# Grouped-query attention: V in 8 KB rows, PV in 64x64 tiles, and another pairing of the heads

## The chip, the cores and the metric

The kernel runs on one core of one Trainium2 chip. The metric is device time in microseconds (us) of one launch; less is better. The kernel is bound to data that comes from memory (HBM) into the on-chip SBUF over 16 DMA engines, and works on five engines: TensorE (PE, matmuls and transposes into PSUM), VectorE (DVE), ScalarE (ACT), GpSimd (POOL) and SyncE (SP, which issues the DMAs here).

## The reference

Attention with grouped queries. There are 16 batches, 8 key/value heads each with 2048 positions of 128 elements, and 32 query heads with 16 positions; four query heads share a key/value head, so 64 query rows meet each K and V head.

```python
B, Hq, Hkv, Sq, Sk, D = 16, 32, 8, 16, 2048, 128      # all bfloat16
k = jnp.repeat(k, rep, axis=1)                        # rep = Hq // Hkv = 4
v = jnp.repeat(v, rep, axis=1)
scale = D ** -0.5
scores = jnp.einsum("bhqd,bhkd->bhqk", q, k) * scale
p = _softmax(scores, axis=-1)
return jnp.einsum("bhqk,bhkd->bhqd", p, v)
```

K and V are 64 MB each and are read once; Q and the output are 2 MB each.

## The kernel before

The 128 key/value heads are taken in 64 pairs, p = 0 to 63. A pair has 2 x 64 query rows, which fill the 128 partitions of a score tile.

**Loads (SP, L180 to L225).** `load_k` brings a pair's K as one DMA of 1 MB: 128 rows of 8 KB, so that partition a of a head holds 32 consecutive positions (`Kn`, six buffers). `load_v` brings a pair's V as 128 partitions x 2 heads x 4 KB (`Vb`, eight buffers), the last pair in two halves. `load_q` brings Q for four pairs in rows of 1 KB, `store` writes 32 KB of output in rows of 256 B. One loop over t issues in order K(t), Q, V(t-5), output(t-12). Each issue waits in this order on SP for its buffer: K for `sem_kt` (K transposed), V for `sem_pv` (PV done), a store for `sem_nm` (output normalized).

**DVE (L338 to L370).** For each pair it turns the score tile into `Sneg` with the row's minimum of the negated scores (L360, `tensor_scalar`), takes the reciprocal of a row sum (`recip`, L351), and transposes the K of two pairs ahead in 32x32 blocks into `KT` (L342, two instructions of 1024 columns).

**PE (L227 to L336).** A program written out by hand (`pe_prog`, L119 to L141): in step p come the scores of pair p+1 ("S", L273 and L232, 32 matmuls of 512 columns in 32x64 tiles, the second half of them on weights that are already loaded), PV of pair p-3 ("PV", L301, 32 matmuls of 128 columns in 128x64 tiles), the transposes of P of pair p ("PT", L284, eight of 128x128), and in two steps of four the transposes of Q ("QT", L251). Eight steps form the body of a loop of seven rounds; four steps before it, three after it and the tail are written out. The waits are on semaphores, in the loop against registers (`at`, `v_at`). Scores have one PSUM tile of four banks (`S_ps`), so S(p+1) waits for DVE's pass over S(p) (`sem_max`). P and Q transposes have three PSUM banks (`ST_ps`), one of them for Q alone.

**ACT (L372 to L411)** follows `act_prog`: exp of pair p (L390, which writes P and the row sum), the normalizing copy of the output of pair p-3 (L410, "norm"), two copies of transposed P into `PT` (L400, "pe"), and copies of transposed Q (L380, "qe").

**POOL (L164)** builds the identity tiles and spreads each Q load into `Q4` (L175).

**The end.** After the loop and three more steps, the tail orders PV 60, PV 61, exp 63, PV 62, the transposes of P 63, PV 63 and the last norms (L131 to L141).

Of the kernel before, what the change touches and what calls it, by code (L numbers as in the profile page):

```python
# [11 lines left out]
NK = 6  # L12
NV = 8
NKT = 2
NPT = 4
NO = 8
NQ = 2
QPAIRS = 4
BODY = 8
VLAG = 5  # L20
PVLAG = 3
SLAG = 12
QLEAD = 7


def bass_standalone__gqa_softmax__sampling_kernel(
# [5 lines left out]
):  # L32
    B, Hq, Sq, D = q.shape
# [3 lines left out]
    G = B * Hkv  # L37
    NP = G // 2
    J = Sk // 128
    assert J == 16 and NP % BODY == 0 and BODY % (2 * QPAIRS) == 0  # L40
    NQC = NP // QPAIRS
# [7 lines left out]
    ident = sb("ident", [128, 128], BF16)  # L49
    ident4 = sb("ident4", [128, 128], F32)  # L50
    Kn = [sb(f"Kn{i}", [128, 2 * J * 128], BF16) for i in range(NK)]
    Vb = [sb(f"Vb{i}", [128, 2, J, 128], BF16) for i in range(NV)]
    KT = [sb(f"KT{i}", [128, 2 * J * 64], F32) for i in range(NKT)]
    Qn = [sb(f"Qn{i}", [128, QPAIRS, 128], BF16) for i in range(NQ)]
    Q4 = sb("Q4", [128, QPAIRS, 2, 4, 64], BF16)
    QT = [sb(f"QT{i}", [128, 2, 128 * QPAIRS], F32) for i in range(2)]
    Sneg = [sb(f"Sneg{i}", [128, Sk], F32) for i in range(2)]
    P = [sb(f"P{i}", [128, Sk // 2], F32) for i in range(2)]
    PT = [sb(f"PT{i}", [128, J // 2, 128], F32) for i in range(NPT)]
    Osb = [sb(f"O{i}", [128, 128], BF16) for i in range(NO)]  # L60
    nbias = sb("nbias", [128, NP], F32)
    rowsum = sb("rowsum", [128, NP], F32)
    rrec = sb("rrec", [128, NP], F32)

    S_ps = ctx.enter_context(nc.psum_tensor("S_ps", [128, Sk], F32))
    ST_ps = ctx.enter_context(nc.psum_tensor("ST_ps", [128, 3 * 512], F32))
    O_ps = ctx.enter_context(nc.psum_tensor("O_ps", [128, 512], F32))
# [4 lines left out]
    sem_vl = [sem(f"sem_vl{i}") for i in range(2)]  # L72
# [10 lines left out]
    sem_ev = sem("sem_ev")  # L83
    sem_nm = sem("sem_nm")

    qf = q.rearrange("b h s d -> (b h s) d")
    of = out.rearrange("b h s d -> (b h s) d")
    kf = k.rearrange("b h s d -> (b h s d)").rearrange("(n a x) -> n a x", n=NP, a=128)
    vf = v.rearrange("b h s d -> (b h) (s d)").rearrange("g (a x) -> a g x", a=128)
# [3 lines left out]
    stages = []  # L93
# [5 lines left out]
    def q_part(c, b):  # L99
        u = stage("Q", c, b)  # L100
        pe_prog.append(("QT", c, b, u))
        act_prog.append(("qe", c, b, u))

    def pv(p):
        pe_prog.append(("PV", p))

    def norm(p):
        act_prog.append(("norm", p))

    def transposes(p):  # L110
        for h in range(2):
            u = stage("P", p, h)
            pe_prog.append(("PT", p, h, u))
            act_prog.append(("pe", p, h, u))

    step_at = {}
    for b in range(2):
        q_part(0, b)
    pe_prog.append(("S", 0))  # L119
    for p in range(NP - 1):  # L120
        step_at[p] = len(pe_prog)
        pe_prog.append(("S", p + 1))
        act_prog.append(("exp", p))
        if p >= PVLAG:
            pv(p - PVLAG)
            norm(p - PVLAG)
        transposes(p)
        c, i = divmod(p, QPAIRS)
        if c + 1 < NQC and i < 2:
            q_part(c + 1, i)  # L130
    tail_at = len(pe_prog)  # L131
    for p in range(NP - 4, NP - 2):
        pv(p)
    act_prog.append(("exp", NP - 1))
    for p in range(NP - 4, NP - 2):
        norm(p)
    pv(NP - 2)
    norm(NP - 2)
    transposes(NP - 1)
    pv(NP - 1)  # L140
    norm(NP - 1)  # L141
    last_q = {what[1:]: u for u, what in enumerate(stages) if what[0] == "Q"}
    last_p = {what[1:]: u for u, what in enumerate(stages) if what[0] == "P"}

    first = PVLAG + 1
    rounds = (NP - 1 - first) // BODY
    assert first % QPAIRS == 0
    after = first + rounds * BODY
    loop_from, loop_to = step_at[first], step_at[first + BODY]
    assert after + 3 == NP - 1  # L150

    def stage_ap(what):
        x = what[2] if what[0] == "P" else 2
        return ST_ps[:, 512 * x:512 * (x + 1)]

    def o_ap(p):
        if p < NP - 3:
            return O_ps[:, 0:128]
        x = p - (NP - 3)
        return S_ps[:, 512 * x:512 * x + 128]  # L160

    with nc.Block() as block:

        @block.gpsimd  # L164
        def _(gp):
# [3 lines left out]
            gp.tensor_scalar(ident4[:, :], iota_t[:, :], 0.0, None, op0=ALU.is_equal).then_inc(sem_id, 1)  # L169
            for c in range(NQC):  # L170
                gp.wait_ge(sem_q[c % NQ], 16 * (c // NQ + 1))
                if c >= 1:
                    gp.wait_ge(sem_st, last_q[c - 1, 1] + 1)
                src = Qn[c % NQ][:, :, :].rearrange("p j (b x) -> p (j b) x", b=2)
                gp.tensor_copy(  # L175
                    Q4[:, :, :, :, :].rearrange("p j b r x -> p (j b) r x"),
                    src.unsqueeze(2).to_broadcast([128, 2 * QPAIRS, 4, 64]),
                ).then_inc(sem_q4, 1)

        @block.sync  # L180
        def _(sp):
            def load_k(p):
                s = p % NK
                if p >= NK:
                    sp.wait_ge(sem_kt, p - NK + 1)
                sp.dma_start(Kn[s][:, :], kf[p]).then_inc(sem_k[s], 16)  # L186

            def load_v(p):
                s = p % NV
                if p >= NV:  # L190
                    sp.wait_ge(sem_pv, p - NV + 1)
                if p < NP - 1:
                    dst = Vb[s][:, :, :, :].rearrange("a g j d -> a g (j d)")
                    sp.dma_start(dst, vf[:, 2 * p:2 * p + 2, :]).then_inc(sem_v[s], 16)
                    return
                for x in range(2):
                    dst = Vb[s][:, :, 8 * x:8 * (x + 1), :].rearrange("a g j d -> a g (j d)")
                    src = vf[:, 2 * p:2 * p + 2, 1024 * x:1024 * (x + 1)]
                    sp.dma_start(dst, src).then_inc(sem_vl[x], 16)
# [9 lines left out]
            def store(p):  # L209
                s = p % NO  # L210
                sp.wait_ge(sem_nm, p + 1)
                sp.dma_start(of[128 * p:128 * (p + 1), :], Osb[s][:, :]).then_inc(sem_o[s], 16)  # L212

            for t in range(NP + SLAG + 1):
                if t < NP:
                    load_k(t)
                for c in range(NQC):
                    if t == max(c, QPAIRS * c - QLEAD):
                        load_q(c)
                if 0 <= t - VLAG < NP:  # L220
                    load_v(t - VLAG)
                if 0 <= t - SLAG < NP:
                    store(t - SLAG)
            for s in range(NO):
                sp.wait_ge(sem_o[s], 16 * (NP // NO))  # L225

        @block.tensor  # L227
        def _(pe):
            pe.wait_ge(sem_id, 3)
# [10 lines left out]
            def emit(op, at, v_at):  # L240

                if op[0] == "QT":
                    _, c, b, u = op
                    if b == 0:
                        pe.wait_ge(sem_q4, at(QPAIRS * c, QPAIRS))
                    if u == 1:
                        pe.wait_ge(sem_ev, 1)
                    dst = stage_ap(op)
                    src = Q4[:, :, :, :, :].bitcast(F32).rearrange("p j b r c -> p j b (r c)")
                    for j in range(QPAIRS):  # L250
                        ins = pe.transpose(dst[:, 128 * j:128 * (j + 1)], src[:, j, b, :], ident4[:, :])  # L251
                    ins.then_inc(sem_st, 1)
                elif op[0] == "S":
                    _, p = op
                    pe.wait_ge(sem_kt, at(p + 1))
                    if p >= 1:
                        pe.wait_ge(sem_max, at(p))
                    c, i = divmod(p, QPAIRS)
                    if p == 0:
                        pe.wait_ge(sem_ev, last_q[0, 1] + 1)  # L260
                    kt = KT[p % NKT][:, :].bitcast(BF16).rearrange("p (t b y e) -> p b e t y", t=J // 2, b=2, e=2)
                    qt = QT[c % 2][:, :, :].bitcast(BF16).rearrange("p b (n e) -> p b e n", e=2)
                    for acc in range(4):
                        b, e = divmod(acc, 2)
                        for u in range(2):
                            for r in range(4):
                                rows = slice(32 * r, 32 * (r + 1))
                                g, h = divmod(r, 2)
                                s_ap = S_ps[64 * g:64 * (g + 1), 512 * (2 * h + u):512 * (2 * h + u + 1)]
                                w = qt[rows, b, e, 128 * i + 64 * g:128 * i + 64 * (g + 1)]  # L270
                                x = kt[rows, b, e, 4 * u:4 * (u + 1), :]
                                if u == 0:
                                    ins = pe.matmul(s_ap, w, x, start=(acc == 0), stop=(acc == 3))  # L273
                                else:
                                    ins = matmul_on_loaded(s_ap, w, x, (32 * r, 64 * g), acc == 0, acc == 3)
                    ins.then_inc(sem_s, 1)
                elif op[0] == "PT":
                    _, p, h, u = op
                    if h == 0:
                        pe.wait_ge(sem_exp, at(p + 1))  # L280
                    dst = stage_ap(("P", p, h))
                    for t in range(4):
                        x = 4 * h + t
# [156 lines left out]
```

## Time and profile before

| what | value |
|---|---|
| three timed runs | 342.7, 342.88, 344.7 us; median 342.88 us |
| profiled execution: its own time, its span | 344.2 us, 342.4 us |
| busy: PE, DVE, ACT, POOL | 82%, 86%, 78%, 9% of the span |
| DMA | 138.63 MB, mean 405 GB/s, 38433 packets |
| K loads | 64 of 1024 KB, 15.9 us from issue to landing (median) |
| V loads | 63 of 1024 KB, 16.5 us; 2 of 512 KB, 12.4 us |
| Q loads, stores | 16 of 128 KB, 15.3 us; 64 of 32 KB, 15.4 us |
| PE waiting for V in front of PV | 36.6 us in 40 waits |
| DVE waiting for K in front of the transpose | 27.8 us in 41 waits |
| granted TensorE clock | 0.994 on average |

The span reaches from the first to the last instruction. In the profile an engine line gives busy time, its share of the span and the number of instructions; the slice line gives the busy share of 40 equal slices in tenths (9 is 90% or more); a timeline line gives start, duration, engine, line of the kernel, operation, output and inputs, and in brackets how long the engine had been idle and what ended that idle time. "SPq" is an issuing instruction on SP.

### The profile page before, as it was taken

What the parts mean: (1) busy time and instruction counts of PE and PEld (TensorE: products, weight loads), DVE (VectorE), ACT (ScalarE), POOL (GpSimd) and SP (SyncE); (2) the same over time, 40 slices, a digit from 0 to 9 for tenths busy, and PEclk for the clock granted to TensorE, in tenths of its full rate; (3) what the DMA queues carried; (4) which work ended last, traced back from release to release, by engine and by line L of the source; (5) the groups of instructions that cost most, each with busy time, mean ns of one, the idle gap of its engine ahead of it and who ended that gap; (6) DMA issues with size and microseconds to landing.
All of it is one profiled execution on the core that took longest, in us unless ns stands there. A gap on an engine that the chain in (4) does not pass through costs nothing.

```text
span 342.4 us, 9887 instructions
## 1 busy us (share of the span) xinstructions
PE 279.9 (82%) x4736; PEld 162.4 (47%) x3712; DVE 295.1 (86%) x320; ACT 267.2 (78%) x353; POOL 31.8 (9%) x23
## 2 busy tenths in 40 slices
PE   0677999999999978879788788878879778798785
PEld 0133555555455644535544544535536445455454
DVE  2489999999999998898898888988988979988940
ACT  1178889999888978878788697796887778787792
POOL 3202020202010010202002020020200102000000
PEclk9999999999999999999999999999999999999997
DMA  7999999999999999999999999999999999999993
GB/s 296 421 409 415 415 408 413 416 413 418 413 415 421 413 418 416 412 419 418 412 421 412 417 417 416 418 417 417 414 419 415 418 414 416 420 419 416 414 409 107
DMA packets 38433, 138.63 MB, mean 405 GB/s; under 512 B 11536, under 2 KB 13584, under 8 KB 30224
## 3 DMA queue, kind: packets, MB, share of 16 engines
q1 hardware_dynamic: 38416, 138.43, 100.0%
q8 instruction: 8, 0.13, 0.2%
q14 instruction: 9, 0.07, 0.1%
HBM read 136.31 MB, written 2.10 MB: 404 GB/s over the span
## 4 chain that ended last, share of the span: by engine, by line
DMA 53%; DVE 20%; issue 9%; SPq 8%; PE 8%; ACT 2%; POOL 1%
DMA Vb<-in_v_dram 47%; DVE KT L342 13%; DVE Sneg L360 6%; SPq L186 6%; DMA Kn<-in_k_dram 5%; PE O_ps L301 3%; SPq L212 2%; PE S_ps L273 1%; DMA Qn<-in_q_dram 1%; PE S_ps L232 1%; ACT O L410 1%; PE S_ps L301 1%; PE ST_ps L251 1%; PE ST_ps L284 1%; POOL Q L175 1%
## 5 line engine op out<-in xcount | busy, mean ns | idle before, releaser
L342 DVE STREAM_TRANSPOSE KT<-Kn 128x1024 f32<-128x1024 f32 x128 | 151.4, 1222 | 27.8 <-DMA Kn<-in_k_dram 27.8
L390 ACT ACTIVATE P<-Sneg,nbias 128x2048 bf16<-128x2048 f32 x64 | 159.6, 2494 | 6.3 <-DVE Sneg L360 6.3
L360 DVE TENSOR_SCALAR_CACHE_REDUCE Sneg<-S_ps 128x2048 f32<-128x2048 f32 x64 | 144.4, 2256 | 7.9 <-PE S_ps L232 7.9
L273 PE MATMUL S_ps<-KT,QT 32*64 32x512 bf16 x1024 | 106.0, 395 | 8.0 <-DVE Sneg L360 6.2
L232 PE MATMUL S_ps<-KT,QT 32*64 32x512 bf16 x1024 | 105.0, 388 | 0.0
L301 PE MATMUL O_ps<-Vb,PT 128*64 128x128 bf16 x1952 | 66.2, 221 | 36.6 <-DMA Vb<-in_v_dram 36.6
L301 PEld LDWEIGHTS O_ps<-Vb,PT 128*64 128x64 bf16 x1952 | 56.5, 110 | 78.8 <-issue 43.9
L400 ACT ACTIVATE PT<-ST_ps 128x512 f32<-128x512 f32 x128 | 69.6, 595 | 20.3 <-PE ST_ps L284 20.3
L284 PE MATMUL ST_ps<-ident,P 128*128 128x128 f32 x512 | 70.8, 282 | 4.1 <-ACT P L390 3.3
L273 PEld LDWEIGHTS S_ps<-KT,QT 32*64 32x64 bf16 x1024 | 32.5, 105 | 72.8 <-issue 62.1
L284 PEld LDWEIGHTS ST_ps<-ident,P 128*128 128x128 f32 x512 | 55.5, 142 | 13.4 <-ACT P L390 9.2
L175 POOL COPY Q<-Qn 128x2048 bf16<-128x2048 bf16 x16 | 30.3, 1896 | 255.6 <-PE ST_ps L251 251.8
L410 ACT ACTIVATE O<-O_ps,rrec 128x128 bf16<-128x128 f32 x61 | 22.5, 369 | 34.1 <-PE O_ps L301 33.9
L251 PE MATMUL ST_ps<-ident,Q 128*128 128x128 f32 x128 | 20.2, 282 | 8.8 <-POOL Q L175 8.1
L380 ACT ACTIVATE QT<-ST_ps 128x512 f32<-128x512 f32 x32 | 19.3, 603 | 8.4 <-PE ST_ps L251 8.4
L251 PEld LDWEIGHTS ST_ps<-ident,Q 128*128 128x128 f32 x128 | 15.5, 145 | 9.1 <-issue 8.0
L390 ACT ACTIVATION_READ_ACCUMULATOR P<-Sneg,nbias 128x1 f32 x64 | 13.2, 207 | 0.0
L351 DVE RECIPROCAL rrec<-rowsum 128x1 f32<-128x1 f32 x64 | 10.2, 159 | 3.0 <-ACT P L390 3.0
L301 PE MATMUL S_ps<-Vb,PT 128*64 128x128 bf16 x96 | 3.9, 243 | 2.7 <-DMA Vb<-in_v_dram 1.6
L360 DVE DVE_READ_ACCUMULATOR Sneg<-S_ps 128x1 f32 x64 | 5.4, 84 | 0.0
L301 PEld LDWEIGHTS S_ps<-Vb,PT 128*64 128x64 bf16 x96 | 3.4, 125 | 3.4 <-issue 2.3
L410 ACT ACTIVATE O<-S_ps,rrec 128x128 bf16<-128x128 f32 x3 | 1.1, 370 | 3.4 <-PE S_ps L301 3.4
(8 smaller groups left out, 3.0 us busy)
## 6 DMA issues: line engine op xcount, KB each, us to landing
Kn<-in_k_dram SPq DMA_DIRECT2D x64, 1024.0 KB, 15.9
Vb<-in_v_dram SPq DMA_DIRECT2D x63, 1024.0 KB, 16.5
Qn<-in_q_dram SPq DMA_DIRECT2D x16, 128.0 KB, 15.3
out_dram<-O SPq DMA_DIRECT2D x64, 32.0 KB, 15.4
Vb<-in_v_dram SPq DMA_DIRECT2D x2, 512.0 KB, 12.4
```

Of the source, the lines that this page charges most:

```text
L175: gp.tensor_copy(Q4[:, :, :, :, :].rearrange("p j b r x -> p (j b) r x"), src.unsqueeze(2).to_broadcast([128, 2 * QPAIRS, 4, 64]),).then_i ...
L186: sp.dma_start(Kn[s][:, :], kf[p]).then_inc(sem_k[s], 16)
L232: return pe.add_instruction(mybir.InstMatmult(name=nc.get_next_instruction_name(), engine=mybir.EngineType.PE, ins=[pe.lower_ap(rhs), pe.l ...
L251: ins = pe.transpose(dst[:, 128 * j:128 * (j + 1)], src[:, j, b, :], ident4[:, :])
L273: ins = pe.matmul(s_ap, w, x, start=(acc == 0), stop=(acc == 3))
L284: ins = pe.transpose(dst[:, 128 * t:128 * (t + 1)], P[p % 2][:, 128 * x:128 * (x + 1)], ident4[:, :])
L301: ins = pe.matmul(o_ap(p)[64 * g:64 * (g + 1), :], pt[:, j // 2, j % 2, 64 * g:64 * (g + 1)], Vb[p % NV][:, g, j, :], start=(j == 0), stop ...
L342: ins = dve.transpose(KT[p % NKT][:, :].rearrange("p (t b e a x) -> p x e t b a", t=J // 2, b=2, e=2, x=2)[:, x, :, :, :, :], Kn[p % NK][: ...
L360: dve.tensor_scalar(Sneg[p % 2][:, :].rearrange("p (t h x) -> p h t x", t=8, h=2), S_ps[:, :].rearrange("p (h t x) -> p h t x", t=8, h=2), ...
L390: act.activation(P[p % 2][:, :].bitcast(BF16).rearrange("p (n y e) -> p n y e", n=16, e=2), Sneg[p % 2][:, :].rearrange("p (n e y) -> p n ...
L400: act.activation(PT[p % NPT][:, 4 * h:4 * (h + 1), :].rearrange("p t q -> p (t q)"), stage_ap(("P", p, h)), ACT.Copy,).then_inc(sem_ev, 1)
L410: act.activation(Osb[p % NO][:, :], o_ap(p), ACT.Copy, scale=rrec[:, p:p + 1]).then_inc(sem_nm, 1)
```

## The change

Two pairs now form a quad d (32 quads of four heads), and a unit u = 2d + i replaces the pair p. Unit i of a quad has the heads {0, 2} (i = 0) or {1, 3} (i = 1) of the quad.

- **K**: the same 1 MB and the same 8 KB rows for a unit, but from two pieces of memory, 64 rows of each of two heads that are not neighbours. One DMA instruction is built by hand whose source is 2 x 64 rows and whose target is 128 partitions. There are seven buffers instead of six. DVE transposes it with one instruction instead of two.
- **V**: a DMA brings two neighbouring heads as 128 rows of 8 KB, so a head lies in 64 partitions. Three buffers of a quad (two loads each) replace eight of a pair. The V of the last quad goes into K buffers that have come free, its last load in rows of 24 and 8 blocks (`LASTJ`).
- **PV**: with a head in 64 partitions, a matmul is 64x64 with 128 columns; there are 128 to a quad, in two halves of 64 in two steps, and the two row halves i write different PSUM banks (`O_ps` has two).
- **P**: exp of the two units of a quad writes interleaved blocks of 64 columns, so that a transpose of 128 columns yields both units. The transposes of a quad follow in two steps, one step later than before; PV follows four steps behind instead of three. P has three buffers of a quad.
- **Q**: 32 loads of 64 KB in rows of 512 B instead of 16 of 128 KB in rows of 1 KB; four transposes and one copy for each. `ST_ps` has two banks instead of three, Q's transposes share a bank with P's, and "QW" is a wait on PE until ACT has copied Q out of it.
- **PE's loop**: six steps in the body, ten rounds, six steps before it; the steps at the end are in the loop too, under branches that skip what isn't there any more. The PV of the last quad follows the loop, in three passes.
- **Output**: a store has 64 partitions x 2 x 256 B; the last quad is normalized by ACT (i = 0) and DVE (i = 1) beside each other.

The core of the diff:

```diff
+NK = 7
+NV = 3
+NO = 6
+NQ = 4
+NQT = 3
+NP = 3
+QPAIRS = 2
+BODY = 6
+FIRST = 6
 VLAG = 5
-PVLAG = 3
-SLAG = 12
+PVLAG = 4
+SLAG = 13
+LASTJ = 24
...
-    kf = k.rearrange("b h s d -> (b h s d)").rearrange("(n a x) -> n a x", n=NP, a=128)
-    vf = v.rearrange("b h s d -> (b h) (s d)").rearrange("g (a x) -> a g x", a=128)
+    of = out.rearrange("b h s d -> (b h s) d").rearrange("(n g i x) d -> n g x i d", n=ND, g=2, i=2)
+    kf = k.rearrange("b h s d -> (b h s d)").rearrange("(n g i a x) -> n i g a x", n=ND, g=2, i=2, a=64)
+    vf = v.rearrange("b h s d -> (b h s d)").rearrange("(n a x) -> n a x", n=NU, a=128)
...
+    for u in range(steps):
+        step_at[u] = len(pe_prog)
+        pe_prog.append(("S", u + 1))
+        if u < NU:
+            act_prog.append(("exp", u))
+        d, half = divmod(u - PVLAG, 2)
+        if u >= PVLAG:
+            pe_prog.append(("PV", d, half))
+            if half and d < ND - 1:
+                act_prog += [("norm", d, i) for i in range(2)]
+        if u % 2 == 0:
+            q_part(u, u // 2 + 2)
+        if u >= 1:
+            d, k = divmod(2 * (u - 1), 4)
+            turn(d, k)
+            if u % 2 == 0:
+                pe_prog.append(("QW", u // 2 + 2))
+            turn(d, k + 1)
...
+        if op[0] == "QW":
+            return [(sem_eq, op[1] + 1)]
...
+            def load_k(m):
+                s = m % NK
+                if m >= NK:
+                    sp.wait_ge(sem_kt, m - NK + 1)
+                sp.add_instruction(mybir.InstDMACopy(
+                    name=nc.get_next_instruction_name(), engine=mybir.EngineType.SP,
+                    ins=sp.lower_ap_dma(kf[m // 2, m % 2]), outs=sp.lower_ap_dma(Kd[s][:, :].unsqueeze(1)),
+                    queue="qSPDynamicHW", mode="Copy", cce_op=ALU.bypass,
+                )).then_inc(sem_k[s], 16)
...
+                d, g = divmod(p, 2)
+                s = d % NV
+                if d == ND - 1:
+                    sp.wait_ge(sem_kt, NU - NK + 2 + g)
+                elif d >= NV and g == 0:
+                    sp.wait_ge(sem_pv, 2 * (d - NV) + 2)
+                for x, (lo, hi) in enumerate([(0, J)] if p < NU - 1 else [(0, LASTJ), (LASTJ, J)]):
+                    dst = v_ap(d, g)[:, lo:hi, :].rearrange("a j d -> a (j d)")
+                    ins = sp.dma_start(dst, vf[p][:, D * lo:D * hi])
+                    ins.then_inc(sem_v[s] if d < ND - 1 else sem_vl[g + x], 16)
...
+            def pv(d, js, gs=(0, 1)):
+                pt = PT[d % NP][:, :, :].bitcast(BF16).rearrange("p t (q e) -> p t e q", e=2)
+                for j in js:
+                    for g in gs:
+                        for i in range(2):
+                            rows = slice(64 * i, 64 * (i + 1))
+                            ins = pe.matmul(
+                                o_ap(d, i)[64 * g:64 * (g + 1), :],
+                                pt[rows, j // 2, j % 2, 64 * g:64 * (g + 1)],
+                                v_ap(d, g)[rows, j, :],
+                                start=(j == 0), stop=(j == J - 1),
+                                skip_group_check=True,
+                            )
+                ins.then_inc(sem_pv, 1)
...
+                    with ExitStack() as inner:
+                        if missing(x):
+                            inner.enter_context(pe.If(it < rounds - missing(x)))
+                        for y, got in zip(range(x, to), held):
+                            for s, n in got:
+                                pe.wait_ge(s, n)
+                            if pe_prog[y][0] == "PV" and got:
+                                pe.nop(nofuse=True)
+                            emit(pe_prog[y])
...
+            pe.wait_ge(sem_max, NU)
+            pe.wait_ge(sem_ev, 2 * NU)
+            for g, js in ((0, range(J)), (1, range(LASTJ)), (1, range(LASTJ, J))):
+                pe.wait_ge(sem_vl[g + (js[0] > 0)], 16)
+                pv(d, js, (g,))
...
-                for g in range(2):
-                    kt(p, g)
+                dve.transpose(
+                    KT[u % 2][:, :].rearrange("p (b j a) -> p j b a", b=2, j=J),
+                    Kd[u % NK][:, :].bitcast(F32).rearrange("p (j b c) -> p j b c", b=2, c=32),
+                ).then_inc(sem_kt, 1)
...
+                    dst = P[d % NP][:, :].bitcast(BF16).rearrange("p (n i y e) -> p i n y e", n=16, i=2, e=2)[:, i]
...
+            for g in range(2):
+                rows = slice(64 * g, 64 * (g + 1))
+                act.wait_ge(sem_pv, 2 * d + 1 + 2 * g)
+                if g == 0:
+                    act.wait_ge(sem_o[d % NO], 32 * (d // NO))
+                act.activation(Osb[d % NO][rows, 0, :], o_ap(d, 0)[rows, :], ACT.Copy,
+                               scale=rrec[rows, 2 * d:2 * d + 1]).then_inc(sem_nm, 1)
```

## The prediction

> **What bounds the kernel.** I read the page's busy shares and slices first, then its DMA issues, then the timeline of a step in the middle, last the timeline of the end.
>
> ```profile
> PE 279.9 (82%) x4736; PEld 162.4 (47%) x3712; DVE 295.1 (86%) x320; ACT 267.2 (78%) x353; POOL 31.8 (9%) x23
> ...
> DMA  7999999999999999999999999999999999999993
> ...
> q1 hardware_dynamic: 38416, 138.43, 100.0%
> ...
> Vb<-in_v_dram SPq DMA_DIRECT2D x2, 512.0 KB, 12.4
> ```
>
> No compute engine is full, but the DMA engines are in every slice but the first and the last. The step in the middle says the same: what starts a step is data landing.
>
> ```profile
> 204.78 2.25 DVE L360 TENSOR_SCALAR_CACHE_REDUCE Sneg<-S_ps 128x2048 f32<-128x2048 f32 x1
> ...
> 205.11 1.09 PE L301 MATMUL O_ps<-Vb,PT 128*64 128x128 bf16 x32 [0.94 <-DMA Vb<-in_v_dram]
> 206.13 1.09 PE L284 MATMUL ST_ps<-ident,P 128*128 128x128 f32 x8
> ...
> 207.59 2.37 DVE L342 STREAM_TRANSPOSE KT<-Kn 128x1024 f32<-128x1024 f32 x2 [0.47 <-DMA Kn<-in_k_dram]
> ```
>
> PV waited 0.94 us for V, the K transpose 0.47 us for K. Such steps take 5.1 to 5.2 us; between 28 and 46 us, where buffers were still ahead, the chain of waits shows K transposes 4.5 us apart (28.20, 32.74, 37.27, 41.81), the pace of DVE. So compute has 0.6 us to spare in a step. The end is another regime:
>
> ```profile
> 321.56 2.37 DVE L342 STREAM_TRANSPOSE KT<-Kn 128x1024 f32<-128x1024 f32 x2 [0.43 <-DMA Kn<-in_k_dram]
> ...
> 331.09 2.46 ACT L390 ACTIVATE P<-Sneg,nbias 128x2048 bf16<-128x2048 f32 x1
> ...
> 334.65 1.72 PE L301 MATMUL S_ps<-Vb,PT 128*64 128x128 bf16 x32 [1.61 <-DMA Vb<-in_v_dram]
> ...
> 336.30 1.97 PE L284 MATMUL ST_ps<-ident,P 128*128 128x128 f32 x8
> ...
> 338.95 1.09 PE L301 MATMUL S_ps<-Vb,PT 128*64 128x128 bf16 x32 [0.69 <-ACT PT L400]
> ...
> 340.08 0.37 ACT L410 ACTIVATE O<-S_ps,rrec 128x128 bf16<-128x128 f32 x1 [1.18 <-PE S_ps L301]
> ```
>
> The last K landed at 321.5 us, the last V at 337.1 (issued at 324.6, 12.5 to landing, as in the page's row of 512 KB issues), the end came 5.3 us later. PV of 1.72 us instead of 1.09 is the granted clock: it stood at 0.5 from 334.9 to 338.3 us, after PE had idled 1.6 us.
>
> **Part 1, the packets (the gain).** The trace's DMA packet records give, by size, the usual length of a record and the commonest distance from start to start on one engine:
>
> ```
> 8192 B: 8207 packets, 309 ns, 306 apart
> 4096 B: 16128 packets, 159 ns, 155 apart
> 1024 B: 2048 packets, 46 ns, 42 apart
>  256 B: 8192 packets, 18 ns, 14 apart
> ```
>
> All four lie on 4.7 ns + bytes / 27.2 per ns. From 100 to 300 us the 16 engines had 3200 us; taking off 4954 packets of 8192, 1152 of 1024, 4896 of 256 B and some 1990 semaphore writes leaves 157.8 ns for each of 9825 packets of 4096. A V pair cost 256 x 157.8 / 16 = 2.525 us; in 8 KB rows, which K shows at 306.3, it costs 128 x 306.3 / 16 = 2.450. Saved: 0.075 x 64 = 4.8 us. The low bound takes 155.4 for the short packet: 2.3 us. I take 4.8, the rate the middle really ran at. Q goes from 2048 packets of 1 KB to 4096 of 512 B, by the line 23.5 ns each: 5.4 to 6.0 us, +0.6. Sixteen more DMAs write 256 more semaphore packets of 9 ns: +0.1. Stores keep 8192 packets of 256 B. Net **-4.1 us** (bounds -1.6 and -4.1): the last V lands at 333.0. Up to the last K 58 V pairs have passed: 4.35 - 0.7 = 3.6, so it lands at 317.9.
>
> K keeps 8192 packets of 8 KB, but one DMA now reads two pieces: its source counts 2 x 64 rows, its target 128 partitions. In this trace all transfers count 128 on both sides and land with 16 increments, one for each engine. I take the same for K; the other case is a rival.
>
> **Part 2, PV in 64x64 tiles.** Per step 64 matmuls of 128 columns instead of 32. In the trace the two column halves start together, 55.7 ns from pair to pair (0.89 us for 32). The new group has four tiles, two of them in the other row half, writing another bank. Nearest row: the scores, where four 32x64 tiles, two to a column half and in different banks, start within 10 ns, and four matmuls of 512 columns take 0.225 us together. So the four go together: 0.89 us again; the other bound is row halves taking turns, 1.78. PE's step now: scores 1.81, PV 0.95, eight transposes 0.95, Q 0.26 (0.53 every second step) = 4.0 of 5.1. Hidden by the wait for V, so 0; without that cover, up to 0.9 x 64.
>
> **Part 3, waits and control.** QW holds the second transposes of an even step until ACT has copied QT out (0.6 us): behind exp (2.5 us) on ACT, in front of the two PT copies there, and behind it on PE stand four transposes and the next scores. In an even step V lands about 3.0 us after the last minimum; PV 0.9, QT 0.5, PT 0.5, the copy 0.6 and PT 0.5 end at about 5.6 and the scores at 7.5, while DVE's next transposed K is ready at 8.0. So 0. About ten compares per six steps: the old loop's COMPARE_BRANCH took 0.21 us (190.06 us) while PE was in its transposes; bounds 0 and 0.4 us a step, hidden in the same 0.5 us; I take 0. One K transpose of 2048 columns for two of 1024 (2.27 us the pair) and exp into an interleaved P cost what they did, with unchanged element counts.
>
> SP: V of an even pair waits for PV of step t-6, and K(t+1), the next V and a store queue behind it on SP. When it passes, at least three K and two V are still on their way: 5 x 2.45 = 12 us of DMA work. In the trace issue to landing was 16 us. So the queue doesn't run dry: 0. The last quad's V goes into K buffers free since K 58 and 59, long before: 0. The start is bound by DMA from 2.3 us on in both: 0.
>
> **Part 4, the end.** From the last K's landing to the end of the last exp the instructions are the same: 321.5 to 333.6 = 12.1 us, so 330.0. Then all hangs on PE and ACT: transposes 0.95 (331.0; ACT meanwhile does two norms and two copies, to 331.9), PV of half a quad 0.95 (332.0), transposes (333.0), PV (333.9, their copies beside it). V is there by then. The last PV has two passes of one g each, so only two tiles at a time: 64 pairs x 55.7 = 3.6 us (337.5). From the last PV to the end took 2.36 us (340.04 to 342.4): 339.85. PE again idles some 2.3 us before the last exp, so the half clock may come again: 0 to 1.7 us for one window of 3.4 us; I take 0.8. End at **340.6**, where before it was 342.4. V's DMA gains 4.1 us and the end behind it grows from 5.3 to 7.6.
>
> **The sum** is against the span of 342.4 us of the profiled execution, whose own time was 344.2; the runs' median is 342.88. -1.8 on the median: **341.1 us**. Its own range: 340.3 (full clock) to 342.0 (a whole window at half clock).
>
> **Rivals.**
>
> *Packets save less* (chance 0.15): the extra 2.4 ns of a 4 KB packet come from something else, such as traffic between the engines. For: most records stand at 155. Against: K's records in the same stretch have no such tail. 58 pairs then save 2.1 - 0.7 = 1.4 us, the last K lands at 320.1, the end comes at 342.8: 343.3 us. The change then does not do what it says.
>
> *A cleaner end* (0.22): the clock stays up, and the engines land together. In the trace the 16 increments of a load come within 0.65 us until 28 us and spread over 1.9 to 2.6 us after a 16 KB instruction packet fell to one engine. If the new program avoids that, 340.6 - 0.8 - 1.9 = 337.9, so 338.4 us. Against: PE's program is no shorter, so the packets should come again.
>
> *Row halves take turns* (0.14), the slower side: PV takes 1.8 us; PE needs 1.81 + 1.85 + 0.95 + 0.26 = 4.9, and the trace shows 0.15 to 0.2 us of turnaround at each of two or three changes of tile shape: 5.3 against 5.13 of DMA, 0.17 x 64 = 11 us on top of the forecast: 352 us. It decides from a PV of about 1.4 us on. Against: the scores' four tiles.
>
> *K on two engines* (0.04): if the split follows the outer count of 2, two engines carry 8192 packets: 8192 x 306 / 2 = 1253 us, and with their sixteenth of the rest (some 175 us) about 1430 us. Such a split was the case in no transfer here. [...]
>
> **How the numbers follow.** Forecast 0.45, less saved 0.15, cleaner end 0.22, turns 0.14, two engines 0.04. A measurement of this kernel can tell about 1% from no change, here 339.5 to 346.3. Faster is the cleaner end, 0.22; same the forecast and its weak form, 0.60; slower 0.18. The range goes from 337.5 to 348, the latter a PV of some 1.6 us; outside are two engines, half of the turns and a few hundredths below.
>
> **Signs.** Right: 8 KB V packets 306 apart, all slices of DMA full, PV groups of four 56 ns apart, PE still waiting for V, the last K at about 318 us and V at 333, then 7 us of PE and ACT. Wrong: idle DMA slices in the middle, PV over 1.4 us a step, PE waiting for ACT's QT copy without V being late, K landing spread over 20 us, or an end within 4 us of the last V.

## The result, and the profile after

The changed kernel takes 1553.0 us (median of 4 runs, 1551.9 to 1554.9) where the kernel before takes 342.8 us beside it: 4.525 times the time, 95% interval 4.509 to 4.541. The profiled execution took 1551.94 us with a span of 1550.0 us. The forecast of 341.1 us was wrong, and so was its range. The rival "K on two engines", which had a chance of 0.04 and was worked out at 1430 us, names what happened. (Medians are over all runs of a kernel, ratios over its undisturbed runs alone, so below the two can differ by a per cent.)

The page of the kernel after, in the parts shown of the kernel before (busy shares, clock and DMA slices, the queue, the chain that ended last, the first group):

```profile
PE 394.7 (25%) x6784; PEld 217.2 (14%) x5760; DVE 294.0 (19%) x258; ACT 271.1 (17%) x353; POOL 34.3 (2%) x38
...
DMA  1122223222232322222222232222322323222243
...
q1 hardware_dynamic: 31504, 138.42, 26.6%
...
DMA Kd<-in_k_dram 66%; SPq L241 10%; SPq L232 7%; SPq L251 5%; SPq L217 3%; DMA Qn<-in_q_dram 3%; DVE KT L388 2%; DVE Sneg L403 0%; PE S_ps L276 0%; PE O_ps L276 0%; PE ST_ps L329 0%; PE S_ps L320 0%; PE S_ps L286 0%; POOL Q L206 0%
...
L388 DVE STREAM_TRANSPOSE KT<-Kd 128x2048 f32<-128x2048 f32 x64 | 147.9, 2311 | 1239.3 <-DMA Kd<-in_k_dram 1239.3
```

The bytes and nearly all busy times are those of before (DVE 294 us, ACT 271 us); PE is longer because much of it runs at a lower granted clock (0.618 on average, 0.994 before). New is that the DMA slices stand at 2 where they stood at 9, that the queue's packets fill 26.6% of the time of 16 engines, and that DVE waits 1239.3 us for K, 80% of the span. The transfers set the end in both kernels, but now most of the engines that carry them are idle.

The timeline of a step in the middle:

```profile
698.25 2.31 DVE L388 STREAM_TRANSPOSE KT<-Kd 128x2048 f32<-128x2048 f32 x1 [19.79 <-DMA Kd<-in_k_dram]
...
721.84 2.31 DVE L388 STREAM_TRANSPOSE KT<-Kd 128x2048 f32<-128x2048 f32 x1 [19.01 <-DMA Kd<-in_k_dram]
...
725.81 1.92 PE L276 MATMUL O_ps<-Vd,PT 64*64 64x128 bf16 x64 [19.38 <-DMA Vd<-in_v_dram]
...
732.03 1.09 PE L276 MATMUL O_ps<-Vd,PT 64*64 64x128 bf16 x64
...
746.12 2.31 DVE L388 STREAM_TRANSPOSE KT<-Kd 128x2048 f32<-128x2048 f32 x1 [19.71 <-DMA Kd<-in_k_dram]
```

A K tile arrives every 24 us (698.25, 721.84, 746.12). Before, it was every 5.1 us. PV in 64x64 tiles, which the forecast had put at risk, takes 1.09 us for its 64 matmuls at full clock, what the 32 of before took.

Two more counts come from the trace's DMA records. Each K load shows three updates of its semaphore (the first load at 1.80, 23.41 and 23.43 us: one early, two as the data lands), where every other transfer shows sixteen. And of the 1550 us, 1217 us have exactly two of the queue's packets under way (its 4-byte semaphore writes left out), and some 154 us have sixteen. **Two engines carry K.** While only they run, one 8192 B packet takes 309 ns (median) on each, 53 GB/s together.

### The profile page after: what moved, and what is told of

Its sections match the earlier page's. It is cut to its first block, busy times and chain, and to the rows that moved or that the text cites. A ratio compares the mean times of both kernels' runs of the same rounds, so it can differ in the third digit from the quotient of the medians.

```text
span 1550.0 us, 14366 instructions
## 1 busy us (share of the span) xinstructions
PE 394.7 (25%) x6784; PEld 217.2 (14%) x5760; DVE 294.0 (19%) x258; ACT 271.1 (17%) x353; POOL 34.3 (2%) x38
## 3 DMA queue, kind: packets, MB, share of 16 engines
q1 hardware_dynamic: 31504, 138.42, 26.6%
## 4 chain that ended last, share of the span: by engine, by line
DMA 69%; SPq 25%; DVE 2%; another core or an unknown queue 2%; PE 1%; issue 1%; ACT 0%; POOL 0%; ACTq 0%; DVEq 0%
DMA Kd<-in_k_dram 66%; SPq L241 10%; SPq L232 7%; SPq L251 5%; SPq L217 3%; DMA Qn<-in_q_dram 3%; DVE KT L388 2%; DVE Sneg L403 0%; PE S_ps L276 0%; PE O_ps L276 0%; PE ST_ps L329 0%; PE S_ps L320 0%; PE S_ps L286 0%; POOL Q L206 0%
## 5 line engine op out<-in xcount | busy, mean ns | idle before, releaser
L388 DVE STREAM_TRANSPOSE KT<-Kd 128x2048 f32<-128x2048 f32 x64 | 147.9, 2311 | 1239.3 <-DMA Kd<-in_k_dram 1239.3
L320 PE MATMUL S_ps<-KT,QT 32*64 32x512 bf16 x1024 | 137.9, 524 | 537.9 <-DVE Sneg L403 537.1
L276 PE MATMUL O_ps<-Vd,PT 64*64 64x128 bf16 x3968 | 91.9, 261 | 552.5 <-DMA Vd<-in_v_dram 382.0
L276 PEld LDWEIGHTS O_ps<-Vd,PT 64*64 64x64 bf16 x3968 | 80.4, 136 | 608.4 <-issue 590.4
L286 PE MATMUL S_ps<-KT,QT 32*64 32x512 bf16 x1024 | 134.9, 511 | 0.0
L320 PEld LDWEIGHTS S_ps<-KT,QT 32*64 32x64 bf16 x1024 | 38.5, 134 | 636.0 <-DVE Sneg L403 320.7
L329 PE MATMUL ST_ps<-ident,P 128*128 128x128 f32 x512 | 91.1, 325 | 9.8 <-ACT P L441 7.9
L329 PEld LDWEIGHTS ST_ps<-ident,P 128*128 128x128 f32 x512 | 72.4, 171 | 24.5 <-issue 20.8
L206 POOL COPY Q<-Qn 128x1024 bf16<-128x1024 bf16 x32 | 33.3, 1041 | 1391.1 <-DMA Qn<-in_q_dram 1391.1
L304 PE MATMUL ST_ps<-ident,Q 128*128 128x128 f32 x128 | 35.6, 433 | 52.0 <-POOL Q L206 52.0
L304 PEld LDWEIGHTS ST_ps<-ident,Q 128*128 128x128 f32 x128 | 22.9, 216 | 60.6 <-issue 30.8
```

The costliest lines, as they stand in the source:

```text
L276: ins = pe.matmul(o_ap(d, i)[64 * g:64 * (g + 1), :], pt[rows, j // 2, j % 2, 64 * g:64 * (g + 1)], v_ap(d, g)[rows, j, :], start=(j == 0) ...
L286: return pe.add_instruction(mybir.InstMatmult(name=nc.get_next_instruction_name(), engine=mybir.EngineType.PE, ins=[pe.lower_ap(rhs), pe.l ...
L304: ins = pe.transpose(dst[:, 128 * x:128 * (x + 1)], src[:, j, b, :], ident[:, :])
L320: ins = pe.matmul(bank, w, kt[rows, b, e, x], start=(acc == 0), stop=(acc == 3))
L329: ins = pe.transpose(dst[:, 128 * t:128 * (t + 1)], P[d % NP][:, 128 * y:128 * (y + 1)], ident[:, :])
L388: dve.transpose(KT[u % 2][:, :].rearrange("p (b j a) -> p j b a", b=2, j=J), Kd[u % NK][:, :].bitcast(F32).rearrange("p (j b c) -> p j b c ...
```

## The experiments

**1. Where the loss is: the K load alone in the kernel before.** The kernel before keeps its V, its PV, its loop; only the K load is the change's (heads are then paired otherwise than its scores expect).

```diff
-                sp.dma_start(Kn[s][:, :], kf[p]).then_inc(sem_k[s], 16)
+                sp.add_instruction(mybir.InstDMACopy(
+                    ... ins=sp.lower_ap_dma(kf[p // 2, p % 2]), outs=sp.lower_ap_dma(Kn[s][:, :].unsqueeze(1)),
+                    queue="qSPDynamicHW", mode="Copy", cce_op=ALU.bypass,
+                )).then_inc(sem_k[s], 16)
```

> The kernel before with nothing changed but the K load, which is the one of the changed kernel (source 2 x 64 rows); heads 1 and 2 of each quad get exchanged in K. Theory (the K load alone carries the loss): two engines have 8192 packets x 306 ns / 2 = 1253 us of K and a sixteenth of the rest, 175 us, at least 1430 us, and near 1550 if what was added on top of that in the changed kernel comes with it. Rival (the loss needs V's rows, the tiles or the order on PE as well): near 343 us.

1535.8 us (1533.8 to 1537.8), 4.480 times the kernel before (4.473 to 4.488). Its page has the same signature:

```profile
span 1536.0 us, 9887 instructions
...
q1 hardware_dynamic: 37520, 138.42, 26.6%
```

One instruction carries the loss. Nothing else of the change is needed for it.

**2. The rest of the change without it: K in one contiguous piece.**

```diff
-    kf = k...rearrange("(n g i a x) -> n i g a x", n=ND, g=2, i=2, a=64)
+    kf = k...rearrange("(n a x) -> n a x", n=NU, a=128)
...
-                sp.add_instruction(mybir.InstDMACopy(...))
+                sp.dma_start(Kd[s][:, :], kf[m]).then_inc(sem_k[s], 16)
```

> The changed kernel with each K load read as in the kernel before: 128 rows of 8 KB in one contiguous piece, so that heads 1 and 2 of a quad stand in each other's place and the scores pair the wrong heads; nothing else differs. This isolates the rest of the change (V in 8 KB rows, 64x64 PV tiles, TensorE loop, last quad's V in K buffers), which the prediction put at 341.1 us. Theory T (all of the loss is in the K load): 341.1 us, 338 to 346, which is a ratio of 0.987 to 1.009; the queue carries over 97% of 16 engines, 8192 B records of 306 to 309 ns. Rival R1 (the V packets save less): 343.3. Rival R2 (cleaner end): 338.4. Rival R3 (row halves of the PV tiles take turns; already spoken against by 64 PV matmuls in 1.09 us at full clock): 352. If it is above 360 us, something beside the K load is slow and the theory is incomplete.

345.9 us (344.4 to 346.3), 1.0068 times the kernel before (1.0044 to 1.0092). The profiled execution took 346.1 us, with a span of 344.3. So the other parts of the change together make it 0.7% slower, inside the forecast's range, and nearer to the rival "packets save less" (343.3) than to the forecast. Its page, then the timeline of its end:

```profile
DMA  7999999999999999999999999999999999999970
...
q1 hardware_dynamic: 32400, 138.43, 98.3%
```

```profile
320.08 2.31 DVE L384 STREAM_TRANSPOSE KT<-Kd 128x2048 f32<-128x2048 f32 x1 [1.13 <-DMA Kd<-in_k_dram]
...
331.68 0.20 ACT L437 ACTIVATION_READ_ACCUMULATOR P<-Sneg,nbias 128x1 f32 x1
...
333.07 1.92 PE L272 MATMUL O_ps<-Vd,PT 64*64 64x128 bf16 x64
...
334.92 1.75 PE L325 MATMUL ST_ps<-ident,P 128*128 128x128 f32 x8
...
337.87 3.58 PE L272 MATMUL S_ps<-Kd,PT 64*64 64x128 bf16 x128 [0.18 <-issue]
```

The queue is full again but for the end. There, after the last K (320.1 us), exp, transposes and PV follow each other as forecast, and the last PV takes 3.58 us, as forecast. How the 345.9 stand to the 341.1 is worked out below.

**3. Is it the number of pieces? K's source as 16 pieces of 8 rows, and as 4 of 32.** The same hand-built instruction; only the outer count of the source changes (both put rows of other heads where the scores expect those of one head).

```diff
-    ... rearrange("(n g i a x) -> n i g a x", n=ND, g=2, i=2, a=64)
+    ... rearrange("(n g i a x) -> n i g a x", n=ND, g=16, i=2, a=8)     # or g=4, a=32
```

> The changed kernel with K's source as 16 pieces of 8 rows in the place of 2 pieces of 64; the load is still one DMA of 128 rows of 8 KB, built by the same instruction. K rows of other heads and positions get into the scores. Theory (the outer count of the source sets the number of engines): 16 engines, 339 to 360 us. Rival (the hand-built instruction or the scattered source is slow as such): 1550 us as it was.

> The changed kernel with K's source written as four pieces of 32 rows instead of two of 64, in one DMA; heads then stand in other places, so scores pair wrong rows. Theory E (the number of engines is the outer count of the source): four engines, 8192 x 306 / 4 = 627 us for K and about 171 for their share of the rest: 800 us; with packets slowed by V's, as with two engines (1553 for 1430), 850 to 950. Rival 16 (two was a special case): 340 to 600 us with 16 engines.

Sixteen pieces: 571.5 us (565.6 to 594.5), 1.661 times the kernel before (1.655 to 1.667). Four pieces: 972.8 us (965 and 980). The DMA slices and the queue's row, sixteen pieces first:

```profile
DMA  8999999999999999999999999999999999999981
...
q1 hardware_dynamic: 32400, 138.43, 99.2%
```

```profile
DMA  2254454535454445445544545354454445455562
...
q1 hardware_dynamic: 31632, 138.42, 47.3%
```

In the run with four pieces four packets are under way in 357 of the middle 587 us; in that with sixteen, sixteen or more nearly throughout. A K load shows five updates of its semaphore with four pieces (one early, four as the data lands) and sixteen with sixteen. So **the outer count of the source set the number of engines** here: 2, 4 and 16 pieces gave two, four and sixteen. Only these three counts ran, and all three divide 128; what another count gives is not shown.

But both times were forecast too low: sixteen engines should have given 339 to 360 us and four 850 to 950. The mean 8192 B record is 548 ns with sixteen pieces and 431 with four, where the kernel before has 312. The engines are there, and something slows packets. With four pieces it does so mainly while V passes: counted 0.15 us after a record's start, 406 of 7485 records are over 500 ns while at most five packets are under way (median 309), and 4698 of 7321 while fifteen or more are. With sixteen pieces 15793 of all 16273 are over 315 ns.

**4. Two DMAs of one head each.** No instruction by hand; sixteen engines carry both (the queue's row below: 99.8% of 16).

```diff
+                for g in range(2):
+                    sp.dma_start(Kd[s][64 * g:64 * (g + 1), :], kf[m // 2, m % 2][g]).then_inc(sem_k[s], 16)
```

> The changed kernel with each K load as two DMAs of 64 rows, one for each head, instead of one DMA with a source of 2 x 64 rows. Theory (the K loads run on two engines, and that is the whole loss): 64 counts on both sides, so 16 engines again; all else as forecast for the change, 341 us, plus 64 more DMAs of 16 semaphore packets, 0.5 us: 339 to 346 us. Rival 1 (the rest of the change costs too: tiles, branches, the wait for the Q copy): 352 us or more. Rival 2 (16 engines that all write one half of the partitions get in each other's way): K at up to half its rate, 157 us more, 400 to 500 us.

578.8 us (566.5 to 594.4), 1.659 times the kernel before (1.656 to 1.662).

```profile
span 564.7 us, 14430 instructions
...
DMA  8999999999999999999999999999999999999991
...
q1 hardware_dynamic: 33424, 138.43, 99.8%
```

The slices say 9 and the share 99.8%, as in the kernel before, but the same bytes take 1.65 times as long: **a busy DMA slice says that packets are under way, not that they are fast**. The mean 8192 B record is 524 ns here. The theory's 339 to 346 us is out; rival 2, engines that get in each other's way, has the direction, but its 400 to 500 us was too low as well.

**5. What slows the packets of K in halves: the partitions that they are written to.** Two versions of the kernel before, each with K in two DMAs of 512 KB from the same places. One writes 64 partitions x 8 KB per DMA, the other 128 partitions x 4 KB (positions then stand in another order than V's).

```diff
-    kf = k...rearrange("(n a x) -> n a x", n=NP, a=128)
+    kf = k...rearrange("(n g a x) -> n g a x", n=NP, g=2, a=128)      # columns alone
...
+                for g in range(2):      # halves
+                    sp.dma_start(Kn[s][64 * g:64 * (g + 1), :], kf[p][64 * g:64 * (g + 1), :]).then_inc(sem_k[s], 16)
...
+                for g in range(2):      # columns
+                    sp.dma_start(Kn[s][:, 2048 * g:2048 * (g + 1)], kf[p, g]).then_inc(sem_k[s], 16)
```

> The kernel before with each K load cut in two DMAs of one head each, of 64 partitions and 8 KB in each: the same 512 KB pieces and the same number of DMAs as in the run with two DMAs that write 4 KB into 128 partitions (347.7 us). Only the target differs. Theory P (engines meet in the partitions that they write): 530 to 620 us, 8192 B records of about 500 ns on average. Rival S (the number of DMAs): 343 to 350 us.

> The kernel before with each K load cut in two DMAs of one head (512 KB) each; each writes all 128 partitions, 4 KB in each, where the whole load wrote 8 KB in each. The positions of a head then stand in another order in the buffer, so scores and V rows don't match. Same bytes from the same places as two DMAs of one head each into 64 partitions, which cost 579 us in the changed kernel. Theory P (what slows those is that engines meet in the partitions that they write): here each engine keeps partitions of its own, 4096 B packets of about 154 to 160 ns, 343 to 350 us. Rival S (it is the number of DMAs, or the source of 512 KB): 500 to 600 us.

Halves: 599.0 us (580.7 and 617.2). Columns: 347.7 us (346.8 to 349.5), 1.0143 times the kernel before (1.0105 to 1.018). The queue's row and the bytes per slice, halves first:

```profile
GB/s 204 222 276 235 217 223 240 222 229 232 215 229 228 217 207 207 216 210 222 210 228 219 226 220 225 228 228 232 229 230 234 231 231 233 229 231 234 229 288 145
...
q1 hardware_dynamic: 39440, 138.43, 100.8%
```

```profile
GB/s 275 414 408 408 405 407 404 408 412 409 413 412 410 414 410 412 411 412 412 410 412 409 414 410 411 412 410 413 413 409 413 410 413 413 413 413 413 412 412 157
...
q1 hardware_dynamic: 47632, 138.43, 101.0%
```

The same pieces and the same number of DMAs: the target makes 225 GB/s or 401 on average. The length of the rows goes with it (8 KB or 4 KB), but is not the cause, since the kernel before moves its K in rows of 8 KB into 128 partitions with records of 312 ns on average, under a queue of 416 GB/s between 100 and 300 us. In the profiled execution with halves (617.2 us) K's 8192 B records take 579 ns on average, and V's 4096 B records, whose load is unchanged, are slowed too (mean 305 ns in the middle 60% of the span instead of 162). As only K's target differs, what is fought over is most likely on the side of SBUF; it hits the transfers that are under way beside K as well. What it is there, no run shows; measured are the two rates. Nor do the halves account for the sixteen pieces of experiment 3: these fill all 128 partitions in one DMA, and their packets are as slow (548 ns). No trace here shows which engine writes which partition, and no run separates that from the scattered source. For the sixteen pieces the cause stays open.

**6. Why 1550 and not 1430: V beside the two engines.** The changed kernel without V's loads of quads 3 to 30 (their PV works on old data).

> The changed kernel without the V loads of quads 3 to 30; PV takes what the first three quads left in its buffers. It asks where the 120 us come from that the changed kernel takes over 1430. Theory A (the two engines carry K and their sixteenth of V, and no packet is slowed): 28 quads x 256 packets / 16 x 306 ns = 137 us less, 1413 us. Theory B (while V's packets run on the other 14 engines, they and K's packets slow each other): the 110 us that the two engines lose go too, 1290 to 1310 us.

1328.7 us (1328.1 to 1329.2), 3.876 times the kernel before. Theory A (1413 us) is out; B (1290 to 1310) is nearer, but some 19 us too low, and no run shows where those go. Two packets are under way for 1200 of the 1327 us, and the mean 8192 B record of the run is 322 ns, where in the changed kernel it is 383. In the changed kernel's trace, counted 0.15 us after a record's start, 8192 B records have a median of 309 ns while at most two packets are active (86 of 7827 are over 500 ns); while nine to fourteen are, 640 of 1067 are over 500 ns, at a median of 609. So V's passage costs the two engines time, not only their own share of V: the run is 224 us shorter, and that share is 137. The rival's sum had no term for it.

**7. A version that keeps the pairing and loads K in one piece.** Unit i of a quad reads row groups 2i and 2i + 1 of two transposed K tiles, so the pairing costs no special transfer. It needs four transposed K tiles, and a loop of twelve steps on PE so that the tile in use repeats with the body.

```diff
-VLAG = 5
+VLAG = 6          # and 8
-BODY = 6
+BODY = 12
-NK = 7
+NK = 6
...
-    KT = [... for i in range(2)]
+    KT = [... for i in range(4)]
...
-            got = [(sem_kt, u + 1)] + ...
+            got = [(sem_kt, u // 2 * 2 + 2)] + ...
...
+                                row = 32 * (2 * i + h)
+                                kt = kts[g]
```

> A version that keeps the pairing of heads {0,2} and {1,3} and loads K in one contiguous piece: the pairing is made in TensorE's reads instead, unit i of a quad reading row groups 2i and 2i+1 of two transposed K tiles. For that four transposed K buffers, K transposed three units ahead, six K load buffers, a TensorE loop of twelve steps, V six loads behind K. Theory T: the time of the run with the contiguous K load, plus up to 4 us for the scores of the second to last unit, which now wait for the last K load, minus what one more V load behind the last K covers: 341 to 346 us. Rival R4 (two tiles that share a row group and differ in column group take turns): the score matmuls double, from about 1.1 to 2.2 us a unit, about 60 us more where TensorE is the bound, 360 to 400 us.

> The same with V eight loads behind K instead of six, so that more of V is still in flight while the last scores and exponentials run. Theory T (the end is set by the chain from the last K landing, about 12 us to the last exp, 7.5 us of transposes and PV, 2.4 us to the end, plus 3 to 4 us for the scores that wait): two V loads of 2.5 us each come out of the time ahead of the last K, so 3 to 5 us less than with six, 337 to 342 us. Rival R5 (the whole is bound by bytes and by a queue that must not run dry, and the later V makes PV wait instead): the same as with six, or up to 3 us more.

390.3 us (388.8 to 393.8), 1.138 times the kernel before (1.134 to 1.142); with V eight loads behind, 388.6 us (382.7 to 393.1), 1.120 times (1.116 to 1.124). Both expectations failed in size; the first lies in the 360 to 400 us of rival R4, but by luck, as shown below. The page, PE's waits and a place in the timeline of the first:

```profile
DMA  8999989999999499999959999995999999686910
...
q8 instruction: 57, 0.93, 0.9%
```

```profile
PE S_ps L319 <- issue: 21.2, 4, 5.4
```

```profile
122.08 0.64 PE L319 MATMUL S_ps<-KT,QT 32*64 32x512 bf16 x4 [5.31 <-issue]
```

The row q8 counts fetched program in packets of 16 KB: 57 over the whole span, against 8 with the loop of six steps. PE idles up to 5.4 us in front of scores, 21.2 us in four waits, although nothing that the profile shows is late. These idles end at 122.08, 190.03, 259.52 and 327.83 us, once in a round of twelve steps, and program packets start in or just before each (115.6 and 119.3 us for the first). That PE waits for its program there is the likeliest reading, argued from these times. It is another cause than the rival named: two score tiles in one row group do not take turns, since at full clock four matmuls still start every 0.225 us (112.97, 113.20, 113.43); eight such groups make 1.8 us a unit, where the rival had taken about 1.1.

The last version goes back to six steps in the loop, with six transposed tiles and, for their room, four K load buffers.

```diff
-NK = 6
+NK = 4
-BODY = 12
+BODY = 6
-    KT = [... for i in range(4)]
+    KT = [... for i in range(6)]
```

> The version with the pairing made in TensorE's reads and V eight loads behind K, with TensorE's loop back at six steps: six transposed K tiles and four K load buffers, so that the tile in use repeats with the loop. Theory F (the 389 us of the twelve-step loop are program fetches: 57 instruction packets of 16 KB spread over the whole span instead of 8, and TensorE idle for no reason that the trace names before scores): about 8 such packets again, no TensorE idle of 5 us, 343 to 349 us. Rival R4 (the scores with two tiles in one row group are slow, or waiting for two K loads is): 370 to 390 us as with twelve steps. Rival R6 (four K load buffers are too few, the queue runs dry): 350 to 370 us, with DMA slices below 9.

363.3 us (360.1 to 365.3), 1.059 times the kernel before (1.054 to 1.063).

```profile
DMA  8978899999999999999999999999999999999761
GB/s 308 416 271 354 340 352 351 394 418 401 379 421 419 421 417 421 416 422 417 417 419 420 417 419 419 421 415 419 420 420 417 419 420 419 421 420 420 260 242 22
...
q8 instruction: 8, 0.13, 0.1%
```

```profile
SPq L217 <- DVE KT L387: 214.3, 60, 6.8
```

Theory F had the program packets right, rival R6 the time (350 to 370 us): the packets are 8 again, no idle of 5 us in front of scores is left, some 21 us are won back by the ratios (1.120 to 1.059 with V eight loads behind), and four K buffers are too few at the start, where SP waits for one to come free (214.3 us in 60 waits over the whole span): six slices of 9 us, the third to the eighth, carry 271 to 394 GB/s instead of 418, which is 9.6 us of transfer. The middle moves 419 GB/s again; the rest of the 17 us over the contiguous version is not worked out. No version of the change that does the whole work beat the kernel before.

**8. Stores as the neighbours that lengthen packets.** The contiguous version without the output's stores but for the last quad's.

> The changed kernel with the contiguous K load, without the stores of the output but for the last quad's. 7936 packets of 256 B at 14 ns leave the queue: 6.9 us of 16 engines. Theory N (the 8 KB records over 315 ns are the neighbours of small packets: they come in bursts where stores and Q pass, in the kernel before on V's 4 KB records, which lie next to the stores, and now on the 8 KB ones): the mean record of 8192 B between 100 and 300 us falls from 311.5 to 309.5 to 310.3, since only Q's small packets are left, and the time is 345.9 - 6.9 - 1 to 2 = 337 to 338.5 us. Rival W (V's source or its 8 KB packets cost it): the mean stays at 311.5, 339 us.

341.8 us (340.7 to 343.3), 0.9957 times the kernel before (0.9931 to 0.9982). Of the 6.9 us that the stores' packets should have freed, 4.1 came (3.8 by the ratios). The mean 8192 B record between 100 and 300 us did not fall; it rose from 311.5 to 314.9 ns. Theory N is wrong, and W, with 339 us, expected no rise either.

## Why the prediction was wrong

**Part 1, K: the step that failed.** "In this trace all transfers count 128 on both sides and land with 16 increments, one for each engine. I take the same for K." All transfers of that trace do count 128 on their slow side, so they could not tell whether the split follows the source's outer count or the target's partitions. The change's source counts 2. Experiments 1 and 3 show that this count decides. K went on two engines, not sixteen, at 53 GB/s, and that is nearly the whole loss: the rest of the change costs 0.7%. A case that no row of the trace covers was taken as the row that looked nearest, and the rival that named the other case was given 0.04.

**The rival's own sum** was 8192 x 306 / 2 = 1253 plus 175 us, 1430 us. It has the mechanism and is 8% short. The first term is near the 1217 us with two packets under way (1200 without V). What it missed is mainly that V's packets and K's slow each other (experiment 6): 24.2 us for a unit instead of 22.3.

**Part 1, V (mis-sized).** By the prediction's own subtraction, 100 to 300 us of the contiguous version leave 307.8 ns for each of 9923 packets of 8 KB (3200 us of 16 engines less 2552 x 23.5 ns of Q, 4923 x 14 of stores and 2173 x 7.7 of semaphore writes, the price that its 157.8 ns implies), not 306.3: 16384 x 1.5 / 16 = 1.5 us less gain. That is the direction of the rival "packets save less", at more than half of its 2.5 us (from 4.1 to 1.6). The rate in the middle rose from 416 to 419 GB/s, less than 1%.

**Part 2: right.** Four tiles go together; 64 matmuls take 1.09 us (experiment 2 and the changed kernel).

**Part 3: right in the main, so far as the contiguous version shows it.** Its rows, V first:

```profile
PE O_ps L272 <- DMA Vd<-in_v_dram: 11.4, 12, 1.6
...
PE ST_ps L325 <- ACT QT L425: 9.9, 29, 0.3
```

The prediction put the wait that QW brings at 0 and counted one without V being late among its signs of being wrong. PE does wait 9.9 us in all for that Q copy (29 times, 0.3 us at most), but under a queue whose slices stay at 9, so little of it can reach the time. SP's queue does not run dry there. The cover is thinner than before, though: PE waits 11.4 us for V instead of 36.6.

**Part 4: right in kind, short in size.** Against the forecast span of 340.6 us the contiguous version has 344.3, and the terms are these. The last K landed at 320.1 instead of 317.9 (320.1 is what the rival "packets save less" had), 2.2 us later: nearly all of the 1.5 us above, and a share of the wider spread, as the sixteen engines end 3.8 us apart instead of 2.4. From there to the end of exp it took 0.3 us less than forecast. From that to the last PV's end it took 9.6 us instead of 8.3 (7.5 and the 0.8 of the half clock): a half-clock window from 332.9 to 336.3 cost 1.5 us where 0.8 was taken, the upper bound being 1.7, and 0.5 us went between the steps. After the last PV it took 2.85 us instead of 2.36. Together 2.2 - 0.3 + 1.3 + 0.5 = 3.7, as measured. The rest of 345.9 - 341.1 is how the sum was set against the median: the profiled execution of before was 1.3 us above its median, that of the contiguous version was not (346.1 against 345.9).

So the likeliest account of this change, even with K on sixteen engines, would have been "slower by 0.7%": a gain of under 3 us in the packets, given back by a longer end and a wider spread. **Open** are what widens the spread, and why 8 KB packets of V and K come at 307.8 ns and, without the stores, at 310.9 by the same subtraction. The middle moves 419 GB/s with the stores and without them, as if something other than the packets' own time held it there; no run here shows where.

## What to carry to other kernels

Before a DMA gets another shape, look at the outer count of its source: here two pieces in one DMA meant two engines (1553.0 us for the kernel), and the updates of its semaphore as the data landed told how many there were (two, four and sixteen for two, four and sixteen pieces). Keep a load's target at all 128 partitions (401 GB/s here against 225 with 64 at a time) and the source of each DMA in one piece (345.9 us against 571.5 with sixteen), and look for another place for a pairing; here TensorE's reads could do it at 419 GB/s in the middle, but no version of that came to the time of the kernel before. Then look at the length of the packets, since full DMA slices hid a factor of 1.65. And where a range hangs on "the same as in all other rows", ask whether any of those rows could have shown the other case.

## What the runs showed of the hardware

- One 1 MB load of 2 x 64 rows of 8 KB ran on two engines at 53 GB/s; 4 x 32 rows ran on four, 16 x 8 and plain 128 rows on sixteen (972.8, 571.5 and 345.9 us in all).
- Sixteen engines were not enough: 8192 B records took 524 to 579 ns on average, against 312, when K went to 64 partitions at a time or as 16 pieces of 8 rows. 4 KB into each of 128 partitions kept 162 ns per 4096 B.
- A slow transfer slowed another beside it: V's 4096 B records went from 162 to 305 ns on average (middle of the span) beside K in halves.
- PE's loop of twelve steps fetched 57 program packets of 16 KB where six steps fetched 8, and PE stood still up to 5.4 us once in a round, 21.2 us in all, most likely for it; the two versions differ by some 21 us, with the change of buffers included.
